# Mixture of experts beside a long convolution: a rewritten head with fp32 logits on four column groups, a written order of the engines, and one filter unit moved into the first expert

## The chip, the cores and the metric

The kernel runs on one core of a Trainium2 chip. TensorE (PE) multiplies, VectorE (DVE) and ScalarE (ACT) work on tiles in SBUF and PSUM, GpSimd (POOL) issues the indirect DMAs and SyncE (SP) the others. The metric is the device time of one execution in microseconds, as the median of several runs. Lower is better.

## The reference, cut to what matters

With x = A_q of 2048 tokens by 512, the output is x plus two branches on the normalized xn.

```python
xn = _layernorm(x, axis=-1)
return x + _A_ref(xn, A_k, A_v, A_shift_k, A_ssm_k, A_ssm_D) + _B_ref(xn, B_w_gate, B_w1, B_w2)
# _A_ref: a causal convolution of 2048 taps per channel, by FFT, of (shifted k) * v; times xn
# _B_ref:
logits = xf @ w_gate                                   # 512 -> 8 experts
topk_idx = jnp.argsort(-logits, axis=-1)[:, :K]        # K = 2
gates = _softmax(topk_val, axis=-1)
for e in range(E):
    w = (gates * (topk_idx == e)).sum(-1, keepdims=True)
    out = out + w * (_silu(xf @ w1[e]) @ w2[e])        # 512 -> 1792 -> 512
```

## The kernel before, in words

The kernel routes the tokens first and then runs the eight experts one after the other, largest first (capacities 576, 552, 540, 528 and four of 512). Each weight slice `wraw` of 512 KB comes over SP's queue into one of three buffers; ACT makes its high part `wh` (L940) and DVE its low part `wl` (L943), and PE multiplies three f32r products for each (L956: wh by xh, wh by xl, wl by xh). The long convolution is done by matrix products for a DFT, cut into units that a planner (`fill`, from the work list `units` in `build`) places between the products of the experts.

**The head.** x comes in eight transfers of 512 KB. For each of four chunks of 512 tokens PE transposes 4 x 4 blocks (L244), ACT evicts them rounded (`xTh`, L245), DVE makes the rest (`xTl`, L246), PE forms eight f32r products with the gate's weights, both parts in 16 columns (L250), ACT evicts them (L253), and PE turns them back (L256). DVE adds the parts into the logits (L262, L263). The statistics of the layer norm (bn_stats L271, bn_aggr L276) stand between. Then follows the routing on DVE: the two largest logits and their one-hots (L344 to L356), counts by PE (L360 to L365), the rank of each expert by its count (L376 to L378), the slot of each token of the first expert (L382 to L391), one-hot tables (L543, L552), and their product on PE (L424), which lists the tokens. From it DVE makes the indices `gix` (L571) for six gathers of raw x rows (`xg`, L878) by POOL. The order of the experts, `perm` (L433 to L438), is read by SP before the first weights can be addressed (L968). A second product (L562) lists each token's scale and offset, DVE scales the gathered rows with them (L917), PE transposes them (`ptx`, L898), ACT and DVE make `xh` and `xl` (L902, L903), and the first expert's products begin. Its 576 tokens are two halves of 288, whose first slice is multiplied half by half.

**The filter units.** The convolution's filter is brought to the frequency domain in eight units (pair 0 or 1 of channels, q8 from 0 to 3): eight transposes of `ks` (L681, L684), four products with `ev` (L618), four evictions (L626, some on DVE, L624), and two writes of 512 KB to `zk_d` (L646). Five of the eight are issued in the head, (0,0) to (0,3) and (1,0); three in the second product of the first expert.

**What sets the order.** A list scheduler orders each engine's instructions by a simulated timeline; `after(late, early, reason)` adds an order where the code wants one. A DMA queue and every engine take their instructions in order. Tiles of one tag share a fixed number of buffers (`b4`: 8, PSUM tags `c` and `mm`: 4 banks and 2 pairs), and a new tile waits until the old one has been read for the last time, by a DMA too. `slots` forms the tables of all other experts (L560, L562, L600) after the first expert has begun.

## Time and profile before

| | us |
|---|---|
| median of 3 runs | 837.88 (836.86 to 840.14) |
| the profiled execution | 844.63 |
| its span | 842.8 |
| PE busy | 821.7 (97%) |
| DVE busy | 477.5 (57%) |
| ACT busy | 356.7 (42%) |
| POOL busy | 152.5 (18%) |

The rows below are of the profiled execution. Busy time counts instructions in execution, and those that overlap once. In a timeline, a bracket at a row's end tells how long the engine was idle ahead of it and what ended that.

### The profile page before, as it was taken

Reading aid. Unit: us, or ns where it says so; the run is one execution under the profiler, and the core shown is the slowest. Engines: PE = TensorE matmul, PEld = TensorE weight load, DVE = VectorE, ACT = ScalarE, POOL = GpSimd, SP = SyncE. Lnnn points to the kernel's source line nnn. Section 1 sums busy time; section 2 is a strip of 40 time slices with the busy share of each in tenths; the row PEclk is TensorE's granted clock in tenths of the full one; section 3 lists DMA queues with packets and bytes.
Section 4 is the critical chain, followed back from the end, with each engine's and each line's share of the span. In section 5 each row is a group of like instructions: output and inputs, shape, how many; then the busy total and the mean of one; then the engine's idle time right before and its main releaser. Section 6 shows DMA issues by size and latency. Waiting matters only on the chain. (4 is left out here: it accounts for less than half of the span.)

```text
span 842.8 us, 14110 instructions
## 1 busy us (share of the span) xinstructions
PE 821.7 (97%) x5532; PEld 683.8 (81%) x5532; DVE 477.5 (57%) x734; ACT 356.7 (42%) x575; POOL 152.5 (18%) x152
## 2 busy tenths in 40 slices
PE   9889999999999999999999989999999999999996
PEld 7569998999999999997978757767777777878885
DVE  6869762679584885246734645635742445335431
ACT  4567434355433553236433346324552245215420
POOL 0110013261303302043100330003100220004221
PEclk9999999999999999999999999999999999999998
DMA  9599759988977765599977595665478996457971
GB/s 344 182 288 352 256 156 271 238 242 242 241 210 175 218 163 184 153 323 220 256 219 223 161 280 192 188 170 183 139 244 257 300 310 184 127 136 238 276 206 63
DMA packets 140097, 185.59 MB, mean 220 GB/s; under 512 B 11633, under 2 KB 107115, under 8 KB 137404
## 3 DMA queue, kind: packets, MB, share of 16 engines
q1 hardware_dynamic: 126364, 150.43, 60.9%
q0 software_dynamic: 13664, 34.23, 14.3%
q8 instruction: 45, 0.74, 0.4%
q14 instruction: 24, 0.20, 0.1%
HBM read 138.47 MB, written 50.63 MB: 224 GB/s over the span
## 5 line engine op out<-in xcount | busy, mean ns | idle before, releaser
L943 DVE TENSOR_TENSOR wl<-wraw,wh 128x1024 fp32r<-128x1024 f32 (+1 forms) x116 | 137.6, 1187 | 184.1 <-ACT wh L940 168.9
L940 ACT ACTIVATE wh<-wraw 128x1024 fp32r<-128x1024 f32 (+1 forms) x116 | 119.6, 1031 | 182.8 <-PE py L1048 77.9
L956 PE MATMUL ps<-xh,wh 128*128 128x512 f32 (+4 forms) x672 | 186.1, 330 | 6.7 <-ACT ht L995 4.6
L956 PE MATMUL ps<-xh,wl 128*128 128x512 f32 (+4 forms) x672 | 183.4, 325 | 0.0
L956 PE MATMUL ps<-xl,wh 128*128 128x512 f32 (+4 forms) x672 | 183.4, 325 | 0.0
L956 PE MATMUL ps<-h,wh 128*128 128x288 f32 (+3 forms) x896 | 153.6, 292 | 0.0
L996 DVE TENSOR_TENSOR h<-ht,h 128x512 fp32r<-128x512 f32 (+4 forms) x112 | 79.0, 709 | 108.1 <-ACT ht L995 101.2
L956 PEld LDWEIGHTS ps<-xh,wh 128*128 128x128 f32 x672 | 113.6, 190 | 31.1 <-ACT ht L995 15.4
L956 PEld LDWEIGHTS ps<-h,wh 128*128 128x128 f32 x896 | 127.6, 188 | 8.7 <-issue 6.4
L994 ACT ACTIVATE h<-ps 128x512 fp32r<-128x512 f32 (+4 forms) x112 | 68.9, 615 | 153.2 <-PE ps L956 141.3
L956 PEld LDWEIGHTS ps<-xh,wl 128*128 128x128 f32 x672 | 113.9, 190 | 10.6 <-issue 1.6
L956 PEld LDWEIGHTS ps<-xl,wh 128*128 128x128 f32 x672 | 113.8, 190 | 8.5 <-DVE xl L903 0.2
L1028 POOL DMA_INDIRECT acc_d<-acc,ids x36 | 43.2, 1201 | 303.2 <-DVE acc L1025 295.6
L956 PE MATMUL ps<-h,wl 128*128 128x288 f32 (+3 forms) x448 | 94.3, 290 | 0.0
L1046 PE MATMUL py<-wh,h 128*128 128x512 f32 x224 | 87.6, 394 | 0.0
L1047 PE MATMUL py<-wl,h 128*128 128x512 f32 x224 | 87.5, 390 | 0.0
L1048 PE MATMUL py<-wh,h 128*128 128x512 f32 x224 | 87.4, 390 | 0.0
L956 PEld LDWEIGHTS ps<-h,wl 128*128 128x128 f32 x448 | 71.2, 189 | 0.8 <-issue 0.8
L995 ACT ACTIVATE ht<-ps 128x512 f32<-128x512 f32 (+4 forms) x112 | 68.3, 611 | 5.8 <-PE pty L1093 3.8
L878 POOL DMA_INDIRECT xg<-xn_d,gix x34 | 35.6, 1047 | 160.8 <-PE ptx L898 95.1
L1012 POOL DMA_INDIRECT acc<-acc_d,gix x36 | 44.3, 1230 | 91.5 <-PE ptx L898 56.5
L1046 PEld LDWEIGHTS py<-wh,h 128*128 128x128 f32 x224 | 42.0, 188 | 15.8 <-issue 6.6
(212 smaller groups left out, 800.0 us busy)
## 6 DMA issues: line engine op xcount, KB each, us to landing
wraw<-in_B_w_dram SPq DMA_DIRECT2D x84, 512.0 KB
wraw<-in_B_w_dram SPq DMA_DIRECT2D x32, 448.0 KB
zk_d<-ev SPq DMA_DIRECT2D x16, 512.0 KB
zv_d<-ev SPq DMA_DIRECT2D x16, 512.0 KB
z<-zk_d SPq DMA_DIRECT2D x16, 512.0 KB
z<-zv_d SPq DMA_DIRECT2D x32, 256.0 KB
zi_d<-zo SPq DMA_DIRECT2D x32, 256.0 KB
zb<-zi_d SPq DMA_DIRECT2D x8, 1024.0 KB
```

Source lines behind the costliest of these rows:

```text
L878: self.gather = nc.gpsimd.indirect_dma_start(out=t[:sb], out_offset=None, in_=self.xn_d[:, :] if r else self.io["A_q"].rearrange("o s d -> ...
L940: w = nc.scalar.activation(hi, raw, AF.Copy)
L943: t = nc.vector.tensor_sub(lo, raw, hi)
L956: self.mm = nc.tensor.matmul(ps[:, u, :n], w, x[:, u, :], start=first and w is wh and k == 0, stop=last and w is wl)
L994: nc.scalar.activation(h, ps[:, :nu, :n], AF.Silu)
L995: acts.append(nc.scalar.activation(t, ps[:, :nu, :n], AF.Silu))
L996: self.hid = nc.vector.tensor_sub(l, t, h)
L1012: nc.gpsimd.indirect_dma_start(out=acc[:sb], out_offset=None, in_=sum_d[:, :], in_offset=bass.IndirectOffsetOnAxis(ap=self.gix[:sb, c0 + b ...
L1028: st = nc.gpsimd.indirect_dma_start(out=sum_d[:, :], out_offset=bass.IndirectOffsetOnAxis(ap=self.ids[:sb, c0 + b:c0 + b + 1], axis=0), in ...
L1046: nc.tensor.matmul(o, a, wh[:, f, :], start=ff == 0, stop=False)
L1047: nc.tensor.matmul(o, a, wl[:, f, :], start=False, stop=False)
L1048: self.mm = nc.tensor.matmul(o, l, wh[:, f, :], start=False, stop=ff == FC - 1)
```

## The change

**Logits.** They are formed in fp32. The weights of 128 input channels stand in one of four groups of 32 columns (8 used, 24 zero), and the four groups of a chunk write to four groups of 32 PSUM partitions; no low part is made. ACT evicts 128 rows, four 128x128 transposes turn them back, and one reduction on DVE adds the four groups. DVE makes two of the last chunk's evictions. Mean and variance are worked out in six steps for all tokens from the raw statistics, ahead of the last reduction, and the square root and the table load stand right behind the logits on ACT.

**Order.** PE, DVE and ACT get a written order for the whole head (`Ordered`: each instruction after the one before it). All of these instructions bear the line of that helper, L146.

**Routing.** The first expert is found by the largest count (`mk`) in place of a full ranking; its number goes to `perm0` through POOL. The product of indices has a PSUM tile of its own (`px`), and `gix` follows it directly. Rank, `perm`, the gate halves and the capacities (17 steps on DVE) stand behind `xlo`, the last low part of the second half's tokens. The number of idle products by which PE is kept busy (`pad`) is changed.

**Filter and queues.** The head issues only pair 0; unit (1,0) goes to the work list. A memset that held the second weight slice until the gathers is gone.

```diff
-WARM = 4
-PADS = 6
+WARM = (5, 4)
+PADS = (6, 4)
...
+
+class Ordered:
+    def __init__(self, builder, engine):
+        self.builder, self.engine, self.last = builder, engine, None
+
+    def __getattr__(self, name):
+        op = getattr(self.engine, name)
+
+        def call(*args, **kw):
+            t = op(*args, **kw)
+            if self.last is not None:
+                self.builder.after(t, self.last, "the written order")
+            self.last = t
+            return t
+
+        return call
...
+        self.dv = self.cp.tile([P, DC], F32, name="dv")
+        nc.sync.dma_start(self.dv, io["A_ssm_D"])
+        self.ks = [self.load_k(cp, 0)]
+        self.ev = cp.tile([P, P], F32, name="ev", bufs=1)
+        nc.sync.dma_start(self.ev, io["c_edge"][:, :P])
         nc.sync.dma_start(rc, io["c_rt"][:, cut:])
+        self.ks.append(self.load_k(cp, 1))
...
-        wg = sp.tile([P, DC, 2, E], F32R, name="wgr")
-        for dc in range(DC):
-            V.tensor_sub(wc[:, dc, :], self.wg[:, dc, :], pb[:, 1, :E])
-        V.tensor_copy(wg[:, :, 0, :], wc)
-        V.tensor_sub(wg[:, :, 1, :], wc, wg[:, :, 0, :])
+        self.pad(pb[:, 0, :P], WARM[0])
+        T.matmul(pb[:, 1, :DC * E], self.ones, self.wg.rearrange("p a e -> p (a e)"), start=True, stop=True)
+        self.pad(pb[:, 0, :P], WARM[1])
+        wc = sp.tile([P, DC, Q], F32, name="wc")
+        nc.gpsimd.memset(wc, 0.0)
+        wm = sp.tile([P, E], F32, name="wm")
+        V.tensor_reduce(wm, pb[:, 1, :DC * E].rearrange("p (a e) -> p e a", a=DC), axis=AX.X, op=ALU.add)
+        V.tensor_sub(wc[:, :, :E], self.wg, wm.unsqueeze(1).to_broadcast([P, DC, E]))
...
+        def products(c):
+            pl = self.pmm.tile([P, 2, D], F32, tag="mm", name="pl")
+            for dc in range(DC):
+                T.matmul(pl[dc * Q:(dc + 1) * Q, 0, :], wc[:, dc, :], xts[c][:, dc, :], start=True, stop=True)
+            pls.append(pl)
+
+        def evict(c):
+            lt = cp.tile([P, 4, DH], F32, tag="b4", name="lt").rearrange("p a b -> p (a b)")[:, :D]
+            A.activation(lt, pls[c][:, 0, :], AF.Copy)
+            lts.append(lt)
+
+        def gather(c):
+            for j in range(4):
+                T.transpose(pls[c][:, 1, j * P:(j + 1) * P], lts[c][:, j * P:(j + 1) * P], self.ident)
+            V.tensor_reduce(self.L[:, 4 * c:4 * c + 4, :],
+                            pls[c][:, 1, :].rearrange("p (j g q) -> p j q g", j=4, q=Q)[:, :, :E, :],
+                            axis=AX.X, op=ALU.add)
...
-                evict = nc.scalar.activation(xh[:, dc, :], pt, AF.Copy)
-                self.low[c, dc] = V.tensor_sub(xl[dc], pt, xh[:, dc, :])
...
-                    nc.tensor.matmul(pl[:2 * E, 0, :], wg[:, dc].rearrange("p a e -> p (a e)"), xt[dc],
-                                     start=k == 0 and dc == 0, stop=k == 1 and dc == DC - 1)
...
+                    turn(c, range(4), dc)
+                    A.activation(xt[:, dc, :], pts[dc], AF.Copy)
+                stats(*range(4 * c, 4 * c + 4))
+                if c < 2:
+                    products(c)
...
+                for dc in range(DC):
+                    if dc % 2:
+                        V.tensor_copy(xt[:, dc, :], pts[dc])
+                    else:
+                        A.activation(xt[:, dc, :], pts[dc], AF.Copy)
...
+        stats(13, 14, 15)
+        products(2)
+        products(3)
+        evict(2)
+        evict(3)
+        gather(2)
+        self.variances(sp)
+        gather(3)
+        self.roots(sp)
...
+    def variances(self, sp):
+        V, st = self.V, self.st
+        rs = self.rs = sp.tile([P, 4, NI], F32, name="rs")
+        V.tensor_sub(rs[:, 0, :], st[:, :, 1], st[:, :, 4])
+        V.tensor_add(rs[:, 1, :], st[:, :, 1], st[:, :, 4])
+        V.tensor_add(rs[:, 2, :], st[:, :, 2], st[:, :, 5])
+        V.tensor_mul(rs[:, 0, :], rs[:, 0, :], rs[:, 0, :])
+        V.scalar_tensor_tensor(rs[:, 2, :], rs[:, 0, :], D / 4.0, rs[:, 2, :], op0=ALU.mult, op1=ALU.add)
+        V.tensor_scalar(rs[:, 2, :], rs[:, 2, :], 1.0 / D, 1e-5, op0=ALU.mult, op1=ALU.add)
...
+        A.activation(self.rstd, rs[:, 2, :], AF.Sqrt)
+        A.activation(self.warm, self.warm, AF.Silu)
...
+        def turn_k(q8, held=None):
+            kt = cp.tile([P, 8, P], F32, tag="b4", name="kt")
+            for i in range(2):
+                pt = self.pc.tile([P, 4, P], F32, tag="c", name="ptk")
+                for u in range(4):
+                    T.transpose(pt[:, u, :], self.ks[0][:, 8 * q8 + 4 * i + u, :], self.ident)
+                A.activation(kt[:, 4 * i:4 * i + 4, :], pt, AF.Copy)
+            return kt
+
+        def pair_k(q8, kt, held=None):
+            evs = [cp.tile([P, 8, P], F32, tag="b4", name="ev") for _ in range(2)]
+            for i in range(2):
+                r = slice(4 * i, 4 * i + 4)
+                ps = [self.pc.tile([P, 4, P], F32, tag="c", name="ps1") for _ in range(2)]
+                for h in (1, 0):
+                    T.matmul(ps[h], self.ev[h * H:(h + 1) * H, :], kt[h * H:(h + 1) * H, r, :], start=True, stop=True)
+                for h in range(2):
+                    self.evicted = A.activation(evs[h][:, r, :], ps[h], AF.Copy)
+            for h in range(2):
+                t = nc.sync.dma_start(self.zk_d[:, 8 * q8:8 * q8 + 8, h * P:(h + 1) * P], evs[h])
+                if held is not None:
+                    held.append(t)
+
+        kts = [turn_k(0), turn_k(1)]
...
+        self.pad(pq[:, 2 * P:3 * P], PADS[0])
+        T.matmul(pq[:, :P], self2d, rt["ones"], start=True, stop=True)
+        T.matmul(pp[:, :P], rt["tri"], self2d, start=True, stop=False)
...
+        self.rstds(0)
+        V.tensor_copy(cs, pq[:, :P])
+        T.matmul(pn[:, :E], cs, rt["pre"][:, P:], start=True, stop=True)
+        T.matmul(pp[:, :P], cs, rt["pre"][:, :P], start=False, stop=True)
+        key, mk, ro0 = t1("key"), sp.tile([P, 1], F32, name="mk"), t1("ro0")
+        V.scalar_tensor_tensor(key, pn[:, :E], float(E), rt["e0"], op0=ALU.mult, op1=ALU.add)
+        V.tensor_reduce(mk, key, axis=AX.X, op=ALU.max)
+        V.tensor_tensor(ro0, key, mk.to_broadcast([P, E]), op=ALU.is_equal)
...
+        V.tensor_mul(pick, ro0[:1], rt["e0"][:1])
+        V.tensor_reduce(pv0, pick, axis=AX.X, op=ALU.add)
+        nc.gpsimd.tensor_copy(self.perm0, pv0)
...
+            T.matmul(pt0, A0[:, i, :], R0[:, i, 0, :], start=i == 0, stop=i == NI - 1)
         tid0 = sp.tile([P, NBLK[0]], F32, name="tid0")
-        self.indexed = self.unpack_tid(pt0, tid0[w], 0, NBLK[0], w)
+        c0 = slice(0, NBLK[0])
+        V.tensor_scalar(self.gix[w, c0], pt0, -1.0, 0.0, op0=ALU.add, op1=ALU.max)
         self.gathers(0)
-        self.rstds(sp)
+        pair_k(1, kts[1], self.held)
+        kts.append(turn_k(3))
...
+        self.rstds(1)
...
+        V.tensor_scalar(tid0[w], pt0, 0.0, float(PAD + 1), op0=ALU.is_equal, op1=ALU.mult)
+        V.scalar_tensor_tensor(self.ids[w, c0], pt0, -1.0, tid0[w], op0=ALU.add, op1=ALU.add)
+        V.tensor_sub(gt, m1, m2)
+        V.tensor_mul(gt, gt, self.rstd)
+        pos = t3("pos")
+        V.tensor_copy(pos.rearrange("p j e -> p (j e)"), pp[:, :P])
+        cnt = t1("cnt")
+        V.tensor_copy(cnt, pn[:, :E])
...
+        pair_k(2, kts[2], self.held)
+        self.ev02 = self.evicted
+        A.activation(gt, gt, AF.Tanh, scale=0.5)
+        pair_k(3, kts[3], self.held)
+        V = nc.vector
+        rk, cap, cb, ov, nb, ex = t1("rk"), t1("capv"), t1("cb"), t1("ov"), t1("nb"), t1("ex")
+        w8 = sp.tile([P, E, E], F32, name="w8")
+        ro = sp.tile([P, E, E], F32, name="ro")
+        self.prep(0)
+        self.after(V.tensor_tensor(w8, b1(key), b2(key), op=ALU.is_gt), self.xlo, "the first expert comes first")
+        V.tensor_reduce(rk, w8, axis=AX.X, op=ALU.add)
+        V.tensor_tensor(ro, b1(rt["e0"]), b2(rk), op=ALU.is_equal)
...
+        V.tensor_copy(self.perm, pv)
...
             t = V.tensor_scalar(gf[:, :, k], gt, 0.5 - k, 0.5, op0=ALU.mult, op1=ALU.add)
-            self.after(t, done, "the tables come first")
+            self.after(t, self.xlo, "the first expert comes first")
...
-        self.after(V.tensor_mul(w8, ro, b1(rt["cap"])), done, "the tables come first")
+        V.tensor_mul(w8, ro, b1(rt["cap"]))
...
-        self.after(V.tensor_mul(w8, rt["low"], b1(nb)), self.xlo, "the first expert comes first")
+        V.tensor_mul(w8, rt["low"], b1(nb))
...
-        if self.nw == 1:
-            self.after(nc.gpsimd.memset(raw[:1, :1, :1], 0.0), self.gather, "the first expert's tokens come first")
         t = nc.sync.dma_start(raw, src)
-        if self.nw == 1:
+        if self.nw == 3:
             for d in self.held:
...
-        ev = nc.sync.value_load(self.perm[0:1, r:r + 1], min_val=0, max_val=E - 1)
+        ev = nc.sync.value_load(self.perm[0:1, r:r + 1] if r else self.perm0, min_val=0, max_val=E - 1)
...
-            units += [("k", lambda q8=q8: self.conv_k(cp, 1, q8)) for q8 in (1, 2, 3)]
+            units += [("k", lambda q8=q8: self.conv_k(cp, q8)) for q8 in range(4)]
...
-    given = dict(inputs, c_edge=edge, c_mid=mid, c_rt=routing_constants())
+    given = dict(inputs, A_ssm_D=np.asarray(inputs["A_ssm_D"]).reshape(DC, P).T, c_edge=edge, c_mid=mid, c_rt=routing_constants())
```

On SP, before, around the first weight slices (`zk_d` are the filter's writes, `wraw` the slices, `perm` the experts' order):

```order
L646 DMA zk_d_58<-ev_395 128x8x128
L646 DMA zk_d_58<-ev_394 128x8x128
L646 DMA zk_d_58<-ev_487 128x8x128
L646 DMA zk_d_58<-ev_486 128x8x128
L968 TENSOR_LOAD perm_86
L968 ISA x2
L930 DMA wraw_863<-in_B_w1_dram 128x4x256
```

Seven more loads of `perm`, left out here, follow this first slice. The changed kernel has at the same place on SP:

```order
L1000 TENSOR_LOAD perm0_87
L1000 ISA x2
L962 DMA wraw_798<-in_B_w1_dram 128x4x256
L962 DMA wraw_864<-in_B_w1_dram 128x4x256
L962 DMA wraw_936<-in_B_w1_dram 128x4x256
L421 DMA zk_d_58<-ev_427 128x8x128
L421 DMA zk_d_58<-ev_428 128x8x128
L962 DMA wraw_1016<-in_B_w1_dram 128x4x256
```

Before, four writes stand ahead of the first slice; now three slices stand ahead of the first write, and the first number is read from `perm0`.

On ACT, before, from the last filter units to the first tokens (`ev` are filter evictions, `wh` the high part of the first slice, `xh` the tokens):

```order
L626 ACTIVATE ev_567<-ps1_569 128x512
L626 ACTIVATE ev_568<-ps1_570 128x512
L626 ACTIVATE ev_568<-ps1_576 128x512
L940 ACTIVATE wh_865<-wraw_863 128x1024
L626 ACTIVATE ev_567<-ps1_575 128x512
L626 ACTIVATE ev_680<-ps1_682 128x512
L626 ACTIVATE ev_680<-ps1_688 128x512
L902 ACTIVATE xh_699<-ptx_707 128x288
```

Two evictions of `ev_680`, of unit (1,0), stand last ahead of the tokens. The changed kernel has at the same place on ACT:

```order
L146 ACTIVATE ev_567<-ps1_569 128x512
L146 ACTIVATE ev_568<-ps1_570 128x512
L146 ACTIVATE ev_567<-ps1_575 128x512
L146 ACTIVATE ev_568<-ps1_576 128x512
L146 ACTIVATE gt_520<-gt_520 128x16
L972 ACTIVATE wh_800<-wraw_798 128x1024
L146 ACTIVATE ev_584<-ps1_586 128x512
L146 ACTIVATE ev_585<-ps1_587 128x512
L146 ACTIVATE ev_584<-ps1_592 128x512
L146 ACTIVATE ev_585<-ps1_593 128x512
L936 ACTIVATE xh_611<-ptx_619 128x288
```

Now eight evictions of units 2 and 3 stand there, four of them behind the high part. `ev_568` takes the buffer of `ev_427`, and `ev_584` that of `ev_428`, which the first two writes on SP read.

On DVE, before, behind the low parts of the second half's tokens (`x` are normalized tokens, `w8` to `en` steps of the routing, `wl` the low part of slice 2):

```order
L299 TENSOR_SCALAR x_106<-x_106,gate_84 128x512
L299 TENSOR_SCALAR x_108<-x_108,gate_84 128x512
L487 TENSOR_TENSOR w8_445<-rt_122,nb_443 128x64
L492 TENSOR_TENSOR iso_786<-pos_589,capv_440 128x128
L488 TENSOR_REDUCE ex_444<-w8_445 128x8
L490 SCALAR_TENSOR_TENSOR dc_784<-ex_444,cb_441 128x8
L529 TENSOR_TENSOR en_838<-ex_444,nb_443 1x8
L943 TENSOR_TENSOR wl_1005<-wraw_1002,wh_1004 128x1024
```

Five routing steps stand ahead of slice 2 here. The changed kernel has at the same place on DVE:

```order
L356 TENSOR_SCALAR x_107<-x_107,gate_84 128x512
L356 TENSOR_SCALAR x_109<-x_109,gate_84 128x512
L536 TENSOR_TENSOR w8_606<-key_395 128x64
L546 TENSOR_SCALAR gf_702<-gt_520 128x16 x2
L537 TENSOR_REDUCE rk_600<-w8_606 128x8
L548 CAST gh_703<-gf_702 128x32
L538 TENSOR_TENSOR ro_607<-rt_123,rk_600 128x64
L549 TENSOR_TENSOR gl_704<-gf_702,gh_703 128x32
L975 TENSOR_TENSOR wl_939<-wraw_936,wh_938 128x1024
L541 TENSOR_TENSOR w9_698<-ro_607,rt_123 1x64
L550 TENSOR_TENSOR w8_606<-ro_607,rt_123 128x64
```

Seven of the moved steps stand ahead of `wl` now and the others behind it, down to `nb`, which `w8_445` read first before.

## Rows read from the trace of the kernel before

**Rows 1.** Busy time by stretch: the stretch in us, its length, then busy us (and instructions) of PE, of the weight loads, of DVE, ACT and POOL, the granted clock, the share of the DMA engines' time and GB/s.

```profile
40.00:54.00 14.00, 10.83 (x59) 6.29 (x56) 9.42 (x41) 9.82 (x19) 5.72 (x7) 0.98 0.78 217
...
57.00:80.00 23.00, 21.73 (x163) 20.90 (x161) 20.30 (x68) 17.25 (x28) 0.59 (x1) 1.00 1.16 367
...
200.00:780.00 580.00, 574.60 (x3943) 467.79 (x3942) 314.90 (x390) 239.16 (x382) 95.92 (x86) 1.00 0.74 212
```

**Rows 2.** Timeline of PE: start in us, time in us, engine, line, operation, out<-in, count.

```profile
45.59 1.53 PE L562 MATMUL pw<-tabR,tabA 128*96 128x24 f32 x16
...
53.81 0.83 PE L956 MATMUL ps<-xh,wh 128*128 128x288 f32 x2
...
59.87 0.53 PE L956 MATMUL ps<-xh,wh 128*128 128x288 f32 x2 [0.25 <-ACT xh L902]
...
80.29 0.70 PE L562 MATMUL ptab<-tabR,tabA 128*128 128x216 f32 x4 [0.28 <-DVE tabR L560]
```

**Rows 3.** Timeline of DVE from the logits to the indices, columns as in rows 2.

```profile
26.68 0.27 DVE L263 TENSOR_TENSOR lgt<-pb,lgp 128x128 f32<-128x128 f32 x1
...
30.22 0.29 DVE L348 TENSOR_TENSOR oh<-rt,tm 128x128 f32<-128x128 f32 x1
...
30.55 0.29 DVE L356 TENSOR_TENSOR sel<-oh 128x128 f32<-128x128 f32 x1
...
34.53 0.17 DVE L389 TENSOR_SCALAR p<-p 128x16 f32<-128x16 f32 x1
...
38.70 0.16 DVE L438 CAST perm<-pv 1x8 int32<-1x8 f32 x1
...
39.46 0.15 DVE L571 TENSOR_SCALAR gix<-pw 96x6 int32<-96x6 f32 x1
```

**Rows 4.** Timeline of PE: four f32r products of the logits, and a burst of a convolution unit on tiles of 64 rows by 32 columns.

```profile
22.46 1.11 PE L250 MATMUL pl<-xTh,wgr 128*16 128x512 f32 x4
...
373.42 1.95 PE L765 MATMUL pu<-z,mid 64*32 64x512 f32 x32
```

**Rows 5.** Timeline of PE: one filter unit in the second product of the first expert, and the products that follow its two parts.

```profile
123.85 1.04 PE L681 MATMUL ptk<-ident,ks 128*128 128x128 f32 x8
...
124.65 0.77 PE L956 MATMUL ps<-h,wh 128*128 128x288 f32 x4
...
128.01 1.99 PE L618 MATMUL ps<-kt,ev 64*128 64x512 f32 x8
...
129.93 0.80 PE L956 MATMUL ps<-h,wh 128*128 128x288 f32 x4
```

**Rows 6.** The first and last gather on POOL and the first two weight slices on SP's queue (timelines), and stretches of a microsecond with the columns of rows 1.

```profile
39.90 1.12 POOL L878 DMA_INDIRECT xg<-in_A_q_dram,gix  x1 [2.46 <-DVE tid L572]
...
46.24 0.92 POOL L878 DMA_INDIRECT xg<-in_A_q_dram,gix  x1 [0.30 <-issue]
...
40.23 8.51 SPq L930 DMA_DIRECT2D wraw<-in_B_w_dram  x2
...
41.00:42.00 1.00, 1.00 (x10) 0.94 (x8) 0.86 (x5) 1.00 (x1) 0.70 (x2) 1.00 0.59 68
...
42.00:43.00 1.00, 0.23 (x3) 0.04 (x2) 0.96 (x9) 0.99 (x4) 0.69 (x2) 1.00 0.92 271
...
43.00:44.00 1.00, 1.00 (x4) 0.64 (x5) 0.44 (x3) 1.00 (x4) 0.69 (x2) 1.00 1.13 408
...
46.00:47.00 1.00, 1.00 (x14) 1.00 (x12) 0.00 (x0) 1.00 (x3) 0.76 (x1) 1.00 0.58 160
...
52.00:53.00 1.00, 0.70 (x4) 0.39 (x4) 1.00 (x2) 0.41 (x1) 0.00 (x0) 1.00 1.14 349
...
54.00:55.00 1.00, 1.00 (x6) 1.00 (x6) 0.87 (x3) 0.93 (x3) 0.00 (x0) 0.50 1.15 349
...
57.00:58.00 1.00, 1.00 (x10) 1.00 (x9) 0.54 (x1) 0.00 (x0) 0.00 (x0) 1.00 1.15 347
```

**Rows 7.** Timelines of ACT (evictions of a filter unit, the table load, the high part of the first slice, an eviction of tokens) and of DVE (the tokens' scaling).

```profile
30.05 2.06 ACT L626 ACTIVATE ev<-ps 128x512 f32<-128x512 f32 x4
...
40.97 1.28 ACT L449 ACT_TABLE_LOAD   x1
...
46.72 1.04 ACT L940 ACTIVATE wh<-wraw 128x1024 fp32r<-128x1024 f32 x1
...
53.07 0.41 ACT L902 ACTIVATE xh<-ptx 128x288 fp32r<-128x288 f32 x1 [0.35 <-PE ptx L898]
...
50.47 1.44 DVE L917 TENSOR_SCALAR xg<-xg,sc,sc 96x512 f32<-96x512 f32 x3
```

**Rows 8.** Timeline of DVE from the routing steps behind the second half's tokens on, and of PE where the low part of slice 3 is first multiplied.

```profile
62.22 0.22 DVE L487 TENSOR_TENSOR w<-rt,nb 128x64 f32<-128x64 f32 x1
...
70.52 0.19 DVE L511 TENSOR_TENSOR f<-f,tq 128x32 f32<-128x32 f32 x1
...
70.62 0.19 DVE L511 TENSOR_TENSOR r<-r,f 128x32 f32<-128x32 f32 x1
...
71.30 0.75 DVE L996 TENSOR_TENSOR h<-ht,h 128x576 fp32r<-128x576 f32 x1
...
73.55 1.22 DVE L943 TENSOR_TENSOR wl<-wraw,wh 128x1024 fp32r<-128x1024 f32 x1
...
77.99 0.42 PE L956 MATMUL ps<-xh,wl 128*128 128x288 f32 x2
```

307 lines of the change are left out of this document (104 added, 203 removed).

## The prediction

> **What bounds the kernel now.** I read the busy time by stage first [rows 1]. From 200 to 780 us PE is busy 574.60 of 580.00 us, so nothing outside PE can give time back there, and every PE instruction that is added costs its full slot. From 57 to 80 us PE is busy 21.73 of 23.00 and DVE 20.30: two engines near their limit at once. Only the head, before the first expert's weights meet its tokens, has PE idle (10.83 busy of 14.00 between 40 and 54). Then I read the timeline of PE for the moments that mark the stages [rows 2]: the product of the scales begins at 45.59, the first expert's matmul at 53.81 (call it T1), its second half at 59.87, and the first product of a routing table at 80.29. That last row says that PE had waited 0.28 us for DVE, so there DVE has no slack at all. Moving T1 forward by a microsecond is worth a microsecond, as long as nothing behind it is late.
>
> **What the change gains in the head.** Logits first. Before, DVE makes 16 low parts and finishes the logits at 26.68 + 0.27 = 26.95 [rows 3]. The new form has no low parts, and of the last chunk DVE takes two plain evictions. My own schedule by the durations of the trace (transposes 0.11, an eviction 0.5, bn_stats 0.6, a small DVE step 0.21) ends at 24.35, with DVE as the last: the statistics and six variance steps stand ahead of the last gather. Bounds: 23.3 if DVE is never late, and 27 if nothing is gained.
>
> Do four column groups really run side by side? In the trace 32 passes of 64x512 on tiles 64x32 take 1.95 us [rows 4], four rounds of 0.49 for eight tiles each. So a chunk of four fp32 products, two passes each, should take about 0.9 us, against 8 f32r products before, four of which take 1.11 us with their ends, so about 2 us. The switch of tile form has a price: the unit of rows 5 holds 4 products, its slot is 129.93 - 128.01 = 1.92 us, while its four rounds take 1.72, so 0.2 us for in and out. Four such switches in a row at worst, 0.8 us, are inside my 24.35 by half. [...]
>
> The chain to the indices is 12.66 us long now (26.95 to 39.46 + 0.15) [rows 3]. It loses the two rank steps for one maximum (0.3), the add behind row 34.53 (0.21), one of three floor steps (0.21), the copy of the positions ahead of the indices (0.21), and some of the wait for the counts (0.3): 1.2 in all. So the indices come at 35.8 instead of 39.61. The expert's number was ready at 38.86 and its first slice issued 1.37 us later, at 40.23 [rows 3, 6]; now it is made by two steps beside the floor, and I put the issue at 34.1.
>
> The product of the scales stood behind filter products whose banks ACT had to free, while ACT loaded a table (1.28 us at 40.97, [rows 7]). It now follows the indices' product directly: about 38.2 to 39.6. The scales follow at 41.1, and the tokens of the first half, scaled from 50.47 to 51.91 before [rows 7], are done by 42.7. If nothing else were late, T1 would come at about 46.1: one filter unit's evictions, the first slice's high part and the tokens' evictions stand between on ACT (43.2 to 45.3, then 0.4, then 0.4).
>
> **What is late next.** On SP three slices of 512 KB now go out ahead of the filter's first two writes. On ACT the second eviction of unit 2 goes into the buffer of the first of these writes, and stands ahead of everything that the first expert needs from ACT: its high part, four evictions, the tokens. Durations [rows 6]: by 44 us, 3.7 after its issue, the first slice and a gather have moved (68 + 271 + 408 = 747 KB); alone the queue moves about 349 GB/s (52 to 53 us), 1.5 us for a slice; with gathers beside it both together moved 408, and the gathers alone 160, so the slices keep some 243, 2.2 us each. That gives 37.8 for slice 0, 39.3 for slice 1 and then, since the gathers' data, which join in the 408 of 43 to 44, some 3.3 after their first issue at 39.90, flow from 35.9 + 3.3 = 39.2 on, 41.5 for slice 2 and 43.7 for the write. Then ACT needs three evictions (1.55), the high part (1.04), four evictions (2.06) and a token eviction (0.4) [rows 7], and T1 comes at 43.7 + 5.1, about 49.0 with 0.2 for signals. Gain 4.8 instead of 7.7. Bounds: 46.1 (the write is in time) and 51.8 (it gets through only when the sixth gather has landed, at about 45, so at 46.7).
>
> [...]
>
> The clock: PE was granted 0.50 at 54 to 55 and 1.00 from 57 on [rows 6], the lower and the higher level, after a stretch in which it was busy 10.83 of 14.00. Now PE is idle for longer before T1, so I expect the same half-rate stretch and no difference. Bounds: 1.5 us gained if it stays at the higher level (half of 3 us), 1.5 lost if it also falls in the idle 2 us before the counts.
>
> **What it adds behind T1.** First, one filter unit moves from the head into the second product of the first expert. Its price is read from a unit that stands there already [rows 5]: eight transposes 124.65 - 123.85 = 0.80, four products 1.92, so 2.7 us, uncovered, because PE is the bound. Its evictions are on ACT, which has room there.
>
> Second, 17 DVE steps (rank, order of the experts, gate halves, capacities, overflow) move from the head's idle time behind the low part of the second half's tokens. Before, DVE ran 45 steps and one slice from 62.22 to 71.30 [rows 8]; without the slice's 1.14 that is 7.94, or 0.176 a step; neighbours without dependence come 0.10 apart (70.52 and 70.62). At 0.16 the 17 steps are 2.7 us. All that follows on DVE up to the first table product keeps its order, and that product had no slack, so PE stalls for all of it: 2.7. Bounds: 1.7 (17 x 0.10) and 5.5 (at 0.325, the spacing of 128x128 steps in the top-2 chain, as 30.22 to 30.55). A weight slice whose low part DVE ends at 73.55 + 1.22 is first multiplied at 77.99, which just holds. After the stall DVE has the same list as before, so it isn't paid twice.
>
> **The sum**, against the profiled execution's own 844.63 us (span 842.8 and 1.8 outside): -4.8 + 2.7 + 2.7 = +0.6. That execution stands 6.75 us over the median of the runs, and I carry the difference over: 837.88 + 0.6 = 838.5.
>
> **Rivals.**
> The write is in time: SP's queue drains faster than I think, T1 at 46.1. Then -7.7 + 5.4 = -2.3, 835.6. For it: ACT could reach that eviction only at about 41.9 anyway. Against: 1.5 MB stand ahead of the write, and the gathers share the engines.
> Most of it is gained: the write in time, and the clock stays up (-1.5), and the 17 steps cost 0.10 each (1.7): -7.7 - 1.5 + 2.7 + 1.7 = -4.8, 833.1. For it: most of those steps are 128x8 or 128x64. Against: they depend on each other.
> Slower, by the wait that takes the gathers' place: the write lands only behind the gathers, at 46.7, T1 at 51.8: -2.0 + 5.4 = +3.4, 841.3. The change loses from a landing later than 43.1 on (where the sum is zero), and by more than 0.5% from 47.3 on. For it: write packets come last in one queue. Against: the 243 GB/s worked out above.
> Column groups that don't run side by side: 2.6 us more a chunk, two chunks of it on the path: +0.6 + 5.2 = +5.8, 843.7. Against it stands row 373.42 [rows 4].
>
> **How the numbers follow.** My forecast has 0.45, the write in time 0.17, most gained 0.22, the late write 0.10, serial groups 0.06. A measurement of this kernel can tell 0.5% from no change, 4.2 us, so faster means under 833.7 and slower over 842.1. The first two lie within; of most gained 0.20 counts as faster; the second gives 0.04 by a smaller stall; late write and serial groups give 0.12 slower. So faster 0.24, same 0.64, slower 0.12. The range runs from 832.8 to 842.5, which leaves out little beyond the serial groups; the likeliest case's own is 836.5 to 840.5.
>
> **What would show it.** Logits ready near 24.4 and indices near 35.8; ACT idle ahead of the second eviction of unit 2, ended by a DMA, until about 44; T1 near 49; PE's wait for DVE ahead of the first table product near 3 us where it was 0.28; four filter units in the first expert instead of three, 2.7 us each. I am wrong if PE doesn't wait at the table product, or if T1 comes before 47 or after 51.

## The result and the profile after

The changed kernel took 842.27 us (median of 9 runs, 839.44 to 843.48), the kernel before 836.86 us beside it (9 runs, 835.47 to 840.14). The ratio is 1.006, with a 95% interval of 1.0043 to 1.0077. The prediction was 838.5 us with a range of 832.8 to 842.5: the time lies at the upper end of the range, and on the side of slower, to which I had given 0.12.

The profiled execution of the changed kernel is its fastest run, 839.44 us (span 837.7). First its timeline of PE, with the columns of [rows 2]: the logits, the last filter products of the head, T1, and the first product of a routing table.

```profile
19.41 2.06 PE L146 MATMUL pl<-xT,wc 128*32 128x512 f32 x16
...
44.82 3.22 PE L146 MATMUL ps<-kt,ev 64*128 64x512 f32 x6 [3.09 <-ACT ev L146]
...
49.52 0.53 PE L988 MATMUL ps<-xh,wh 128*128 128x288 f32 x2
...
77.12 0.70 PE L634 MATMUL ptab<-tabR,tabA 128*128 128x216 f32 x4 [2.78 <-DVE tabR L632]
```

Line 146 is the helper that keeps the written order, so in the head one goes by the tiles. The waits in brackets are the two that the prediction spoke of: PE stands 3.09 us for ACT ahead of the last head products, and 2.78 us for DVE at the first table product, where [rows 2] had 0.28. T1 is 49.52 against 53.81 in [rows 2].

The next rows are the indices on DVE and, on ACT, the evictions that wait for the filter's write and, behind it, for PE; they answer to [rows 3] and [rows 7].

```profile
34.57 0.16 DVE L146 TENSOR_SCALAR gix<-px 96x6 int32<-96x6 f32 x1 [0.59 <-PE px L146]
...
44.17 1.57 ACT L146 ACTIVATE ev<-ps 128x512 f32<-128x512 f32 x3 [3.61 <-DMA zk_d<-ev]
...
48.08 1.08 ACT L146 ACTIVATE ev<-ps 128x512 f32<-128x512 f32 x2 [0.31 <-PE ps L146]
```

ACT had 3.61 us of idle time, ended by a DMA at 44.17: that is the write whose landing I had put at 43.7. So far every step is near where it was expected. Now the granted clock. These are stretches of the same execution, with the columns of [rows 1]; the last number but two is the clock.

```profile
20.00:45.00 25.00, 19.98 (x143) 13.66 (x134) 16.45 (x69) 12.34 (x25) 7.22 (x11) 1.00 0.65 222
45.00:49.00 4.00, 4.00 (x14) 2.18 (x14) 1.37 (x2) 3.69 (x8) 0.00 (x0) 0.57 0.20 53
49.00:833.00 784.00, 774.76 (x5275) 649.68 (x5273) 439.77 (x618) 331.70 (x532) 146.66 (x132) 1.00 0.79 220
833.00:837.00 4.00, 0.00 (x0) 0.00 (x0) 0.00 (x0) 0.00 (x0) 0.00 (x0) 0.61 0.18 64
```

From 45 to 49 us PE is busy all the time, at 0.57: in this trace the clock stands at 0.50 from 45.5 to 48.5 us, and at 1.00 from 44 to 45 and from 49 to 50. PE had stood from 41.7 to 44.8. By these numbers the 4.00 us would have been 2.3 at 1.00, so I estimate 1.7 us as lost. The last stretch, behind PE's last product, costs nothing.

Then the kernel before, in a second execution that I took with the experiments (836.21 us, span 834.4), because the one shown ahead of the prediction, 844.63 us, is well over the median. The same view:

```profile
20.00:829.00 809.00, 799.37 (x5425) 666.26 (x5423) 464.73 (x702) 347.09 (x557) 149.56 (x143) 1.00 0.77 221
829.00:834.00 5.00, 0.00 (x0) 0.00 (x0) 0.00 (x0) 0.00 (x0) 0.74 (x1) 0.56 0.14 51
```

and its timeline of PE:

```profile
52.67 0.51 PE L956 MATMUL ps<-xh,wh 128*128 128x288 f32 x2
...
77.75 0.70 PE L562 MATMUL ptab<-tabR,tabA 128*128 128x216 f32 x4 [0.27 <-DVE tabR L560]
```

At 836.21 us, a usual time beside the result and in the first two groups of experiments, the kernel before is at 1.00 from the head to its last product. The stretch behind 54 us that [rows 6] shows at 0.50 isn't in this execution, and T1 is 52.67 where it was 53.81.

Each run also has the mean granted clock of its span. For the kernel before it was 0.997 (mean of 25 runs in the first group of experiments), for the nine runs of the change 0.992. As lost time, one minus the clock times the span, that is 2.5 us against 6.9. The kernel before loses its 2.5 almost all behind its last product (5.00 us at 0.56 are 2.2). The change loses 4.4 us more, beside a difference in time of 5.4; but these are means of two groups of runs, since no clocks are on record for the runs of the kernel before that stand beside the nine. Within one group the change loses 2.5 us more, as the next section shows.

### The profile page after: what moved, and what is told of

Same layout as the page of the kernel before. It is cut to its first block, busy times and chain, and to the rows that moved or that the text cites. A ratio compares the mean times of both kernels' runs of the same rounds, so it can differ in the third digit from the quotient of the medians.

```text
span 837.7 us, 14103 instructions
## 1 busy us (share of the span) xinstructions
PE 816.3 (97%) x5536; PEld 678.2 (81%) x5536; DVE 467.4 (56%) x707; ACT 357.5 (43%) x580; POOL 155.1 (19%) x153
## 5 line engine op out<-in xcount | busy, mean ns | idle before, releaser
L912 POOL DMA_INDIRECT xg<-xn_d,gix x34 | 37.4, 1099 | 158.0 <-PE ptx L932 92.1
```

What stands on the lines that cost most here:

```text
L912: self.gather = nc.gpsimd.indirect_dma_start(out=t[:sb], out_offset=None, in_=self.xn_d[:, :] if r else self.io["A_q"].rearrange("o s d -> ...
```

## The experiments

Two theories stood after the result. **The clock**: the change's path is about as long as before, and the time is lost because PE, idle at new places in the head and at the table, is granted a lower clock behind them (0.57 above). **The path**: the time is lost at the two new waits themselves, the write at 44 us and the table product at 77, and in the moved unit; the clock is a by-product. Kernels run in four groups; a ratio is always to the kernel before in the same group.

The starts of ACT's high part of a weight slice mark the stages. The table gives them as differences from the second execution of the kernel before, in us; slices are counted from 0, and a minus is earlier.

| slice, start before | after | write first | steps back | idle products | write, steps and products | unit moved in before |
|---|---|---|---|---|---|---|
| 1, 53.27 | -3.06 | -4.76 | -1.74 | -5.05 | -5.87 | -0.72 |
| 2, 59.45 | -3.14 | -4.66 | 0.00 | -4.87 | -5.52 | +1.02 |
| 6, 83.56 (table product passed) | -0.64 | -0.64 | +0.20 | -0.87 | -5.32 | +1.03 |
| 11, 114.78 | -0.66 | -0.66 | +0.18 | -0.89 | -5.34 | +1.01 |
| 20, 184.47 (moved unit passed) | +2.33 | +2.32 | +3.16 | +2.09 | -2.36 | +4.09 |
| 115, 811.27 | +2.83 | +1.26 | +2.00 | +3.63 | +5.18 | +3.99 |

From slice 11 to slice 20 every kernel of this table that has the fourth filter unit in the first expert loses 2.98 to 3.08 us. That is the price of the unit. The two starts of slice 20, from ACT's timelines, first of the kernel before:

```profile
184.47 1.06 ACT L940 ACTIVATE wh<-wraw 128x1024 fp32r<-128x1024 f32 x1
```

```profile
186.79 1.06 ACT L972 ACTIVATE wh<-wraw 128x1024 fp32r<-128x1024 f32 x1
```

The second is the change's, 2.33 us later (2.32 by these rounded rows); at slice 11 it was 0.66 us earlier.

**Both kernels again.** No edit; before's is the execution shown above.

> The changed kernel, unchanged, once more. Path theory (the time differs by what the two profiles show on PE's path: first matmul 4.3 us earlier, stall at the first table product 2.5 us longer, one unit of 2.7 us more): the same three numbers again within 0.3 us, and a net change near -0.5 to +1 us, so a ratio of 0.999 to 1.001. Clock theory (most runs lose further time because PE falls to the lower clock after its new idle stretches, which the profiled run of after hardly did): ratio 1.004 to 1.008 again, with a mean granted clock of 0.990 to 0.992 where the runs of before have 0.994 or more, each 0.001 of mean clock being worth about 0.84 us.

> The kernel before, unchanged, for a second trace of it. If the trace shown ahead of the prediction is a common execution: lower clock at 53.5 to 56.9 again, and a stop of PE of 3.4 us near 497 again, span near 842. If it was an uncommon one: no lower clock ahead of the last microseconds, no stop near 497, span near 834.5, and every mark from the first table product on about 1.5 us earlier, behind 500 us about 7 us earlier.

Measured for the change: 839.8 us (6 runs), ratio 1.0054 [1.0035, 1.0072], mean clock 0.994, which is above the 0.990 to 0.992 that the clock theory expected. Against the kernel before in this group the mean span is 4.2 us longer, and the time lost to the clock, reckoned as above, is 2.5 us more. Its trace has the same T1 (49.51) and table wait (2.77). ACT waits for the write twice, 1.12 us until 43.28 and 1.20 us until 47.09, and the slow stretches are at other places:

```profile
29.00:33.00 4.00, 4.00 (x11) 1.46 (x11) 3.36 (x15) 1.15 (x3) 0.18 (x1) 0.57 0.00 0
33.00:49.00 16.00, 13.64 (x89) 8.79 (x88) 6.75 (x28) 10.17 (x20) 6.47 (x7) 1.00 0.82 240
49.00:54.00 5.00, 4.98 (x27) 4.65 (x26) 4.05 (x8) 2.31 (x6) 0.00 (x0) 0.66 0.98 278
```

The first follows PE's 1.4 us of waiting for the top-2 choice near 27 us, the second a wait of 1.7 us for ACT ahead of T1. So one trace doesn't tell where a kernel loses its clock; the mean over its runs does better. In these two traces of one kernel the slow stretches are 45 to 49 us (0.57) in one, 29 to 33 (0.57) and 49 to 54 (0.66) in the other.

**The write first.** SP issues unit 0's two filter writes ahead of the first weight slice.

```diff
+                if q8 == 0:
+                    self.first_z = t
...
+        if self.nw == 0:
+            self.after(t, self.first_z, "the filter's first writes come first")
```

> The filter's first two writes go out on SP ahead of the first weight slice; nothing else is changed. Path theory: ACT no longer waits for a write at 40.6 to 44.2, the third gather ends the wait instead, first matmul 2.5 to 3.5 us earlier than in the changed kernel (46 to 47), and the time 2.5 to 3.5 us under it. Rival (the first slice is late now, since 1 MB stands ahead of it): first matmul near 49 as before, no gain. Clock theory: the gain of the path, and 1 to 2 us more if PE then keeps the higher clock into the first matmuls.

Measured: 839.49 us (12 runs), 1.0043 [1.0026, 1.006], clock 0.993. T1 and the table product:

```profile
47.82 0.51 PE L992 MATMUL ps<-xh,wh 128*128 128x288 f32 x2
...
75.59 0.70 PE L636 MATMUL ptab<-tabR,tabA 128*128 128x216 f32 x4 [2.77 <-DVE tabR L634]
```

ACT no longer waits for the write and T1 is 1.7 us earlier, yet by slice 6 the kernel stands where after stands (-0.64). The table product comes 1.5 us earlier than in after, but it still waits for DVE, and behind that wait this trace has a slow stretch, from 77 to 80 us: two products of 288 columns take 0.48 us there from start to start, against 0.26 to 0.28 ahead of the wait and from 80 us on. The 2.5 to 3.5 us that the path theory expected of the time did not come. The write alone isn't the loss.

**The steps back.** 13 of the 17 moved DVE steps stand in the head again, ahead of the third unit's products.

```diff
-        self.after(V.tensor_tensor(w8, b1(key), b2(key), op=ALU.is_gt), self.xlo, "the first expert comes first")
+        V.tensor_tensor(w8, b1(key), b2(key), op=ALU.is_gt)
...
+        pair_k(2, kts[2], self.held)
+        self.ev02 = self.evicted
```

> 13 of the 17 DVE steps (rank, order, capacities, overflow) go back ahead of the first expert, into the time in which DVE waits for gathers and for ACT; the gate halves stay behind. Path theory: PE's wait at the first table product falls from 2.8 to 0.5 to 1.0 us, the first matmul stays at 49.5, and the time is 1.8 to 2.3 us under the changed kernel. Rival (PE's stall is only moved, since DVE is the bound up to 91 us in any case): no gain in time. Clock theory: 1.8 to 2.3 plus up to 1.7 us, if the stall was followed by a stretch at the lower clock in most runs.

Measured: 838.33 us (12 runs), 1.0034 [1.002, 1.0047], clock 0.992. The wait at the table is gone and T1 is later:

```profile
50.87 0.52 PE L988 MATMUL ps<-xh,wh 128*128 128x288 f32 x2
...
77.94 0.70 PE L634 MATMUL ptab<-tabR,tabA 128*128 128x216 f32 x4 [0.44 <-DVE tabR L632]
```

So the moved steps are the cause of the stall (2.78 to 0.44). Both places of the path theory have now been mended once, and neither gives the whole loss back: the steps' ratio is 0.2% under that of the change in this group, with intervals that overlap. The clock stayed at 0.992 and 0.993.

**Both of these together.**

> Both edits together. Path theory: 4.5 to 5.5 us under the changed kernel, so what is left against the kernel before is the unit (2.7) less the earlier first matmul (about 7): 3 to 4 us faster than before by the profiles. Clock theory: the mean granted clock comes back to that of before (0.994 or more), and the time falls by more than the sum of the two edits on the path. Neither: the time stays over that of before, and the loss is somewhere else, behind the head.

Measured: 840.51 us (8 runs), 1.0047 [1.0031, 1.0063], clock 0.992. T1 is 50.32, 2.5 us later than with the write alone; 1.4 of that stand before any of the steps (DVE's first step behind the scales' product starts at 41.76 against 40.33). The steps have a price in the head too: in the trace of the steps alone, eleven of them stand on DVE between 47.7 and 50.2, ahead of the low part of the first slice, which the first expert needs. Here they stand there as well, and PE waits 1.58 us for DVE at 52.73. No better than either.

**Idle products.** The kernel after, with products of ones that nothing reads where PE stands: 12 instead of 6 ahead of the counts, and 12 ahead of the fourth unit's products.

```diff
-PADS = (6, 4)
+PADS = (12, 4)
...
+        self.pad(pq[:, 2 * P:3 * P], 12)
         pair_k(3, kts[3], self.held)
```

> The changed kernel with more idle products on PE and nothing else: 12 instead of 6 ahead of the counts, and 12 ahead of the last filter unit, where PE waits for ACT (41.7 to 44.8). No engine's work on the path is changed, so the path theory expects no difference from the changed kernel within 0.5 us, and it expects the first matmul at 49 to 50. Clock theory: the stretches at the lower clock near 29 us and near 50 us go, the mean granted clock rises from about 0.993 to 0.996, and the time falls by 1.5 to 3.5 us.

Measured: 837.88 us (12 runs) against 836.64 (24 runs), ratio 1.0005 [0.9991, 1.0018] (the medians alone give 1.0015, which lies in the interval), clock 0.9964 against 0.9973. The edit adds only work on PE, and of the 0.5% it leaves nothing that can be measured. The trace is of the slowest of the twelve runs, 839.84 us. Its timeline of PE:

```profile
40.59 2.94 PE L146 MATMUL pw<-ones 128*128 128x128 f32 x24
43.47 1.99 PE L146 MATMUL ps<-kt,ev 64*128 64x512 f32 x8
...
47.54 0.53 PE L989 MATMUL ps<-xh,wh 128*128 128x288 f32 x2
...
75.37 0.70 PE L635 MATMUL ptab<-tabR,tabA 128*128 128x216 f32 x4 [2.79 <-DVE tabR L633]
```

and its clock by stretch:

```profile
20.00:76.00 56.00, 50.92 (x371) 42.46 (x366) 45.07 (x164) 36.20 (x64) 7.88 (x12) 1.00 0.93 277
76.00:81.00 5.00, 5.00 (x28) 5.00 (x28) 5.00 (x11) 1.19 (x2) 0.00 (x0) 0.66 0.55 212
81.00:830.00 749.00, 746.46 (x5061) 622.10 (x5060) 406.59 (x515) 310.34 (x496) 141.80 (x130) 1.00 0.76 216
```

The 3.09 us of waiting are filled by 2.94 us of products, the head is at 1.00 throughout, and eight records of filter products take 1.99 us where six took 3.22. T1 comes 5.13 us ahead of before's 52.67. The one wait that has no products in it, 2.79 at the table, is followed by 0.66.

The experiment isn't clean, though. With the new work on PE the list scheduler also changed the order on SP: the filter's first writes go out behind two slices, where after has three ahead of them. First SP's timeline of after, then of this kernel:

```profile
32.69 1.55 SPq L962 DMA_DIRECT2D wraw<-in_B_w_dram  x3
34.36 2.64 SPq L421 DMA_DIRECT2D zk_d<-ev  x2
```

```profile
32.62 0.99 SPq L963 DMA_DIRECT2D wraw<-in_B_w_dram  x2
33.72 1.72 SPq L421 DMA_DIRECT2D zk_d<-ev  x2
35.64 10.46 SPq L963 DMA_DIRECT2D wraw<-in_B_w_dram  x2
```

ACT's wait for the write ended at 41.55, 2.62 us earlier than in after, and from there to T1 it took 5.99 us against 5.35. So by this chain T1's 1.98 us against after are the earlier write's, not the clock's. The kernel to hold this one against is the one with the write first: its T1 is 47.82 against 47.54, its table wait 2.77 against 2.79, its price of the unit the same 2.98. They differ in the clock, 0.993 against 0.9964, and in the ratio, 1.0043 [1.0026, 1.006] against 1.0005 [0.9991, 1.0018]. (Each ratio is to the kernel before in its own group.)

**Only the moved unit, in the kernel before.** Unit (1,0) goes to the first expert; everything else of before stays.

```diff
-        step((1, 0), shared=True, held=self.held)
+        self.ks1 = self.load_k(cp, 1)
...
-        step((1, 0))
...
+            units += [("k", lambda q8=q8: self.conv_k(cp, 1, q8)) for q8 in range(4)]
```

> The kernel before with one part of the change alone: filter unit (1,0) goes from the head into the first expert. Path theory: the unit costs 2.7 to 3.1 us in the expert; in the head the product of the scales no longer waits for its products and evictions, so the first matmul comes 2 to 5 us earlier, and the sum is between 2 us faster and 1 us slower. Clock theory: as the head loses about 3 us of PE work, the lower clock comes into the stretch around the first matmul in most runs (mean clock 0.995 or less instead of 0.997), and the sum is 1 to 3 us slower than the kernel before.

Measured: 840.55 us (5 runs), 1.0056 [1.0032, 1.0081], clock 0.992. In the same group as the idle products, this one edit makes a loss as large as that of the whole change, and it does so on an old head. First the waits of PE that the unit leaves, then the clock by stretch:

```profile
42.94 2.66 PE L617 MATMUL ps<-kt,ev 64*128 64x512 f32 x8 [1.87 <-ACT ev L625]
...
49.66 2.15 PE L897 MATMUL ptx<-ident,xg 96*128 96x96 f32 x12 [2.61 <-DVE xg L916]
```

```profile
20.00:49.00 29.00, 22.49 (x143) 14.63 (x141) 24.09 (x97) 16.99 (x29) 7.13 (x11) 1.00 0.64 207
49.00:57.00 8.00, 7.32 (x36) 7.05 (x37) 5.48 (x12) 2.26 (x5) 0.00 (x0) 0.57 1.06 327
57.00:830.00 773.00, 768.90 (x5240) 645.18 (x5240) 432.29 (x592) 329.41 (x526) 143.62 (x131) 1.00 0.77 220
```

Eight us at 0.57 are, by the same estimate, 3.4 us lost. The unit was PE's work in the head; with it taken out PE is idle 1.87 and 2.61 us ahead of T1, where the kernel before was idle 0.77 and 0.40 in its second execution, and the first expert starts at 0.57. T1 itself is 51.84, only 0.8 us earlier than before; the unit costs its 3.08 behind it.

**Write, steps and products together.** The write first, 12 products ahead of the counts, and the 13 steps in places where DVE was idle (10 ahead of the scales' product, 3 behind the scales). No products ahead of the fourth unit.

```diff
+        self.stepped = V.tensor_reduce(nb, cmp, axis=AX.X, op=ALU.add)
...
-                if u:
-                    self.after(t, self.xlo, "the first half comes first")
+                self.after(t, self.xlo if u else self.stepped, "the first half comes first")
```

> The changed kernel with the first two filter writes ahead of the slices, 12 idle products ahead of the counts, and 13 of the moved DVE steps back in the head at the places where DVE waits (10 ahead of the scales' product, 3 behind it, and the tokens' scaling strictly behind them). Path theory: first matmul at 47.5 to 48.5, PE's wait at the first table product under 1 us, so the table product about 5 us earlier than in the changed kernel's profile (72 to 73 us after the start), and a time 4 to 5 us under it, near 836 and level with the kernel before. Clock theory: the same, plus a mean clock of 0.995 or more; if the clock stays at 0.992 the time stays near 838.

Measured: 840.17 us (12 runs), 1.0048 [1.0029, 1.0067], clock 0.993. Up to 600 us this is the fastest kernel of the study: T1 46.71, the table wait 0.47, and 2.8 us ahead of before at 560 us, unit included. Then, up to 700 us, it loses 8 us, seven of them behind 597, in the stretch where the second layer's inputs and weights load:

```profile
640.00:650.00 10.00, 7.88 (x34) 5.94 (x33) 5.89 (x7) 3.45 (x4) 0.00 (x0) 1.00 0.53 192
650.00:660.00 10.00, 10.00 (x46) 8.29 (x45) 1.23 (x1) 0.92 (x2) 0.00 (x0) 1.00 0.77 260
660.00:670.00 10.00, 6.92 (x19) 5.20 (x18) 5.09 (x6) 2.83 (x4) 4.98 (x4) 0.66 1.02 263
```

PE stands twice, and behind the second stop the clock is 0.66. The chain of the first stop, from its timeline:

```profile
641.77 1.06 ACT L975 ACTIVATE wh<-wraw 128x1024 fp32r<-128x1024 f32 x1 [16.57 <-DMA wraw<-in_B_w_dram]
...
642.87 0.50 PE L1081 MATMUL py<-wh,h 128*128 128x512 f32 x1 [1.36 <-ACT wh L975]
```

A weight slice landed late. My expectation, that a mended head carries through to the end, was wrong for this kernel.

**The last two groups.** In them the kernel before itself took 844.08 (17 runs, clock 0.994) and 845.18 us (17 runs), with spreads of 10 and 11 us where the first two groups had 3.5 and 4.9; only ratios are read. The first of these kernels is the last one (write, steps and products) again, unchanged.

> The kernel e_fix again, unchanged, for a second trace. Theory (its loss of 8 us between 597 and 700 us belongs to the one profiled execution): the trace shows less than 3 us lost there against the kernel before, and the runs spread as before, 837 to 845. Rival (the kernel loses there always): the trace shows the two PE stops at 641 and 662 us again, each over 2 us, and the median is 840.

Measured: 851.96 us (6 runs), 1.0102 [1.007, 1.0135], clock 0.990. Between slices 84 and 85 (626 to 641 us in before's trace) it loses 3.2 us, as the first trace did (3.3), and from slice 80 to 95 (599 to 694 us) 5.3 us against 7.1. So the loss there isn't an accident of one execution, and the expectation of less than 3 us was wrong. Why the slice lands late in this kernel, while the write alone (-0.3) and the next kernel (0.0) lose nothing at that place, stays open.

**Products and steps, without the write first.** The same without the order for unit 0's writes, and with 12 products ahead of the fourth unit. As with the idle products alone, SP issues these writes behind two slices. (The "first kernel with both mends" of the expectation is the one with write, steps and products.)

> The kernel after with idle products in both places (12 instead of 6 ahead of the table, 12 ahead of the fourth unit's slice) and 13 of the 17 late DVE steps back in DVE's idle time of the head; the write of the first unit stays where it is. Theory (the clock, and the table stall as the rest of the loss): clock 0.996 or more, no PE stop over 1 us at the first table product near 76 us, and 834.5 to 836.5, faster than before by 0.1 to 0.3 per cent. Rival (what is gained ahead of 560 us is lost in the DMA-filled stretch at 600 to 700 us, as in the first kernel with both mends): 838 to 840 at a clock of 0.996.

Measured: 846.17 us (12 runs), 1.003 [1.0004, 1.0057], clock 0.9947 against before's 0.9944. Both it and the kernel above have their T1 within 0.33 us of 49.52, so the head's clock can be compared directly. First the one without products ahead of the fourth unit, then this one:

```profile
20.00:45.00 25.00, 20.82 (x151) 15.03 (x145) 17.16 (x78) 12.38 (x25) 7.38 (x11) 1.00 0.69 217
45.00:53.00 8.00, 8.00 (x36) 6.16 (x34) 6.73 (x14) 5.99 (x13) 0.00 (x0) 0.57 0.61 162
```

```profile
20.00:500.00 480.00, 470.03 (x3740) 419.50 (x3732) 306.24 (x499) 218.93 (x369) 103.90 (x93) 1.00 0.80 227
500.00:506.00 6.00, 4.92 (x15) 3.90 (x16) 3.17 (x5) 3.23 (x6) 0.00 (x0) 0.72 1.00 269
```

Eight us at 0.57 behind a wait of 3.6 us for ACT, against 1.00 up to 500 us. The clock came out as the theory has it, the time didn't: I had expected a ratio under 1, and it is 0.3% above. All three kernels of this group lose 6.8 us from slice 11 to slice 20, where the unit costs 3.0 in the groups before (the last section has what these traces show there). The clock's loss against before is gone; a gain over before wasn't reached.

**Idle products for the moved unit in the kernel before.** 7 and 10 products where the unit left PE idle.

```diff
+        self.idle(pw[:, 0, 2 * P:3 * P], 7)
         step((0, 3))
...
         self.gate_t = self.tabled
+        self.idle(pw[:, 0, 2 * P:3 * P], 10)
```

> The kernel before with its unit (1,0) moved to the first expert, and in the two places that the unit left idle on TensorE (1.87 us ahead of the last head products, 2.6 us ahead of the first expert's transposes) 7 and 10 products of ones that nothing reads. Theory (the clock): the granted clock of the runs goes from 0.992 back to 0.996 to 0.998, the half-clock stretch that the kernel with the moved unit shows from 49.4 to 56.3 us is gone, and the time falls from 840.6 to 836.5 to 838.0. Rival (the moved unit costs its place, the clock is a by-product): 840 to 841 with the clock at 0.996, or the idle products delay the first expert and the time is above 841.

Measured: 852.08 us (6 runs), 1.0105 [1.0074, 1.0137], clock 0.9925. This one missed, by its own making. The products write a tile that DVE reads, so DVE waits for the first batch, and the second batch waits for DVE. First DVE's timeline, then PE's:

```profile
42.96 0.29 DVE L447 COPY pos<-pw 128x128 f32<-128x128 f32 x1 [4.07 <-PE pw L269]
```

```profile
51.03 4.64 PE L269 MATMUL pw<-ones 128*128 128x128 f32 x20 [2.29 <-DVE tb L471]
```

DVE's chain is nearly 4 us later, PE stands 2.29 us ahead of the second batch, and the batch itself runs slowly (0.23 us a record, where 24 took 2.94 above), at a clock of 0.61 from 49 to 53 us and 0.54 from 53 to 57. It says nothing on the theory.

**The unit back in the head of the changed kernel**, as real work for the idle place.

```diff
+        kts.append(turn_k(0, 1))
         pair_k(3, kts[3], self.held)
+        pair_k(0, kts[4], self.held, 1)
...
+            units += [("k", lambda q8=q8: self.conv_k(cp, q8)) for q8 in (1, 2, 3)]
```

> The kernel after with the unit (1,0) back in the head as real work: its 8 transposes stand in TensorE's idle place ahead of the fourth unit's slice, its 8 product records behind that slice; all else as in after. Theory (the path gives the head's gain minus the unit's price, and the idle places cost clock): T1 near 51.5 us (2 later than after's 49.5, some 1.8 ahead of before's 53.3), the 3.0 us that after loses in the first expert's later tables is gone, the mean granted clock of the runs is that of before within 0.001, and the ratio to before is 0.996 to 1.001. Rival (the loss of after is neither the unit nor the clock): the ratio stays at 1.004 to 1.007. Rival (the unit needs buffers that the write at 44 us releases): T1 at 53 or later and a ratio of 1.001 to 1.004.

Measured: 849.39 us (12 runs), 1.005 [1.0023, 1.0077], clock 0.989 against 0.994. The second rival was right about the place. ACT's evictions of the unit wait for a buffer that a write must leave, and T1 is 57.06. First ACT's timeline, then PE's:

```profile
54.49 2.06 ACT L146 ACTIVATE ev<-ps 128x512 f32<-128x512 f32 x4 [3.12 <-DMA zk_d<-ev]
```

```profile
55.14 2.21 PE L934 MATMUL ptx<-ident,xg 96*128 96x96 f32 x12 [2.59 <-ACT ev L146]
57.06 0.83 PE L990 MATMUL ps<-xh,wh 128*128 128x288 f32 x2
```

From slice 11 to 20 it loses 0.09 us against before (by slice 30, at 249 us, 1.27). So the unit's place does cost what the first expert pays for it, but the new head has no room for it behind the write: T1 is 4.4 us later than before's 52.67, and the ratio missed both the 0.996 to 1.001 of the theory and the 1.001 to 1.004 of that rival.

## Why the prediction was right and wrong

**The head** was right. Logits were ready at 23.44 where I had 24.35, the indices at 34.73 where I had 35.8, and T1, put at 49.0, came at 49.52. From the landing of the write to T1 it took 5.35 us on ACT, where I had 5.3. The column groups do run side by side: 16 passes of two chunks in 2.06 us, so the rival of serial groups is out. The landing itself, 44.17 against 43.7, agrees in part by luck: the first slice was issued at 32.69 and not at 34.1, and the write took 11.5 us from there where I had 9.6. (My 243 GB/s for the slices is 248 by its own rows, 408 - 160; that moves nothing.)

**Behind T1** it was right too. The unit was put at 2.7 us and costs 3.0; the DVE lag was put at 2.7 and the wait grew from 0.27 to 2.78, 2.5 us.

**The step that failed** is the clock, a term that I put at nothing: "Now PE is idle for longer before T1, so I expect the same half-rate stretch and no difference." The kernel before at its usual time has no such stretch: it is at 1.00 up to its last product, and the stretch in [rows 6] was one of an execution 6.75 us over the median. In place of no difference, the change loses 2.5 us more to the clock than the kernel before in the same group of runs (0.994 against 0.997). My bound of 1.5 us was also too small: it allowed one stretch, and the second trace of the change has two, at places that the first doesn't have.

**A second error** stands beside it. I saw the 6.75 us and carried them over as a constant ("I carry the difference over"), instead of asking whether the stages I subtract from were themselves late. T1 was: 53.81 against 52.67, so 1.14 us of the gain of 4.8 were never there.

Against the second execution of the kernel before, the terms of the path are 49.52 - 52.67 = -3.15 for T1, +2.5 for the table and +3.0 for the unit, together +2.35; slice 20 stands at +2.33. The slow stretch from 45 to 49 us is hardly in it, since T1 hangs on ACT, which waited 0.31 us for PE there. So the path alone gives about +2.0 to +2.35 and not +0.6: 1.14 by the late T1 of the first trace, 0.5 by T1 itself, 0.3 by the unit, less 0.2 at the table. For the change again, whose mean span is 4.2 us over before's, 2.5 us of clock leave 1.6 for the path. That the measured 842.27 lies in the range, by 0.23 us, is luck: the upper end was drawn for a late write, and not for the clock.

How far this is shown. The table holds each kernel against the kernel before in its group: the mean span, and the time lost to the clock, an estimate from one minus the clock of each run times its span.

| kernel | group | span over before, us | clock loss over before, us |
|---|---|---|---|
| after again | 1 | 4.2 | 2.5 |
| write first | 1 | 3.4 | 3.4 |
| steps back | 1 | 2.8 | 4.5 |
| both of these | 1 | 4.1 | 4.5 |
| idle products | 2 | 0.7 | 0.8 |
| unit moved in before | 2 | 4.5 | 4.5 |
| write, steps and products | 2 | 3.8 | 3.5 |
| the same again | 3 | 8.7 | 4.1 |
| products and steps | 3 | 2.4 | -0.2 |
| unit moved, with products | 3 | 8.2 | 1.7 |
| unit back in the new head | 4 | 4.6 | 3.9 |

In the first two groups the clock accounts for the difference to within 1.7 us for every kernel (for the steps back it is more than the difference). The idle products bring the clock up and the loss away, and against the write-first kernel they do so at the same T1, table wait and price of the unit; taking one unit of PE's work out of the old head brings the clock down to 0.992; mending either wait leaves it at 0.992 and 0.993. What stays open: the idle products also moved a write on SP, after wasn't run in their group, and in the third group something else costs more than the clock.

## What to carry to other kernels

Before terms are subtracted from a profile, its time is to be held against the median; if it is far off, a second trace tells which of its stages are late by accident (here T1, 53.81 against 52.67). A head that is made shorter for other engines can leave TensorE idle just ahead of its busiest stretch, as here for 3.09 us. Waits of 1.4 to 3.6 us were followed by stretches at a mean clock of 0.57 to 0.72 in many of the traces, though not each time (in the first trace of the change the 3.09 was, the 2.78 at the table wasn't), so such places counted as a cost even where nothing else waited. Here they could be filled with products that nobody reads (mean clock 0.9964 with them, 0.993 in the kernel with the write first), if these wrote where no other engine had to read; where DVE read the tile, PE waited 2.29 us for it. And where a scheduler orders the queues, an edit on one engine can move another's work (here idle products on PE moved a write on SP from behind three slices to behind two), so the order on the others is to be looked at before the edit is called the only difference.
